# Two of six blocks by way of DRAM in all groups but the last, the written order up to there, and a last period in an order of its own

## The chip, the cores and the metric

The kernel runs on one core of a Trainium2 chip. The core has a matrix engine (TensorE, PE), a vector engine (VectorE, DVE), a scalar engine (ScalarE, ACT), GpSimd (POOL) and SyncE (SP), which issues nearly all DMAs here. The metric is the device time of one execution in microseconds; lower is better.

## The reference

```python
# attention: B, H, S, D = 4, 8, 768, 64; proj is 64 x 6
q_bucket = sum over 6 bits of (q @ proj > 0) * 2**bit      # k_bucket likewise
scores = q @ k.T / sqrt(D), -1e9 where q_bucket != k_bucket
attn = exp(scores - rowmax);  attn /= attn.sum(-1) + 1e-9
out = attn @ v
# mixture of experts: x = out as 3072 tokens x 512, E = 8, F = 1024
expert = argmax(x @ w_gate);  gate = softmax(x @ w_gate)[expert]
y[token] = gate * (maximum(x @ w1[expert], 0) @ w2[expert])
```

All arithmetic is in float32. A product of two float32 operands runs on the matrix engine in two passes, so a program instruction shows as two records; products of split operands (a high part xh and a rest xl, likewise whi and wlo) run in one.

## The kernel before

**Groups and blocks.** The 32 heads form 16 pairs, each pair two groups: group k = 0 to 31 has 384 queries (three parts jj of 128) of both heads hh of a pair, that is 6 blocks x = 2·jj + hh of 128 queries by 768 keys. A block passes through: S, its scores (PE, L237 and L238); X, the row maximum with the scores copied out (DVE, L248, L249); E, the exponential (ACT, L253); its transpose, keys on the partitions, into a tile `pt`; and the product with V. The transpose has two ways. T is six PE transposes (L277, halves a and b), each half copied from PSUM by K (ACT, L281). Blocks 2 and 3 (`AWAY`) of the groups in `MOVED` take the other: X writes them permuted into `pd`, O writes `pd` to DRAM (`moved`, eight DMAs for both blocks, L263), B reads it back as `pq` (L266), and U transposes it in squares on DVE into `pt` (L269). The part jj = 1 is just the blocks 2 and 3.

**Products with V.** A0, A1 and A2 are the products of a group's three parts, each 12 instructions (24 records, L294), all into one PSUM tile `o`; each part has its own tile pt0, pt1, pt2, of which pt0 has two buffers. Then follow EV (copy of `o`), SU and RC (sums), OT (transposes back, L320) and OM (L331). After the last group of a batch of eight, LG to SC route the batch's tokens: logits, argmax, slots, and a scatter of the token rows by POOL into `xs` in DRAM, grouped by expert.

**The order.** `ORDER` is a list of names with lags: period t emits each name for group t minus its lag, so that each engine's instructions stand in that order. A period emits the products of group t-1 (A0, A2, A1), the transposes of group t, and the scores of group t+1; N0 to N5 mark the six places 6t+n of a period, at which `marker` may add work. The list serves groups 2 to 27 (`START`, `END` = 28; `MOVED` = 2 to 27). Groups 0 and 1 and groups 28 to 31 are written step by step: step i handles block i mod 6 of group i div 6, `steps_of` emitting scores ahead and `PIECES` = {1: "1", 3: "2", 5: "0"} the products of the group before, one part at a time. The last group has code of its own, with the routing of the last two groups and the first products of the expert layer among it.

**Beside it.** For each pair LQ and LV load q, k and v (`qk`, `vt`), Q and K_ split them on POOL, and CP, CT, CR and CW form hash codes (PE, L155; DVE, L160) and copy their rows into q and k by DMA (L188). `prefill` clears an expert's rows of `xs` by one DMA of 910 KB from `zrow` (L122); `FILL` = 3, 5, 7, 9, 11, 23, 35, 47 are its places. At place 166 (`PICK`) the expert that comes first is chosen on DVE. At place 174 `weights_early` closes the pools of the early tiles and opens `wpa` (first expert's weights, whi and wlo) and `xep` (its first rows `xre`, its later rows `xrl`); then come its W1 in four loads of 512 KB (`wraw`), a cast on DVE (L758) and a subtraction on POOL (L761) for each, and four turns of `xre` (DVE, L722). SP issues a load when its `wraw` buffer (two of them) is free again.

**Expert layer.** After the last group, L792 forms the first expert's products: the part of `xre` (y = 0), then that of `xrl` (y = 1), which is loaded late. The other experts follow, double-buffered.

Of the kernel before, what the change touches and what calls it, by code (L numbers as in the profile page):

```python
# [18 lines left out]
P = 128  # L19
# [45 lines left out]
def lsh_attention_moe_kernel(ctx, tc, qkd, q2d, k2d, v, pjbd, wg, w1, w2, ident_in, tri_in, cols_in, eoff_in, ids_in, out):  # L65
# [28 lines left out]
    early, first, psa, in_order = ExitStack(), ExitStack(), ExitStack(), ExitStack()  # L94
    rawp = early.enter_context(tc.tile_pool(name="rawp", bufs=4, side="right"))
    pdp = early.enter_context(tc.tile_pool(name="pdp", bufs=2, side="right"))
    start = ExitStack()
    raw0 = start.enter_context(tc.tile_pool(name="raw0", bufs=2, side="right"))
    wpa = []
# [180 lines left out]
    def half_copy(t, pt, c):  # L280
        A.copy(out=pt[:, 3 * c:3 * c + 3], in_=t[:, 0:384].rearrange("p (c q) -> p c q", c=3))  # L281
# [55 lines left out]
    def route(b, g):  # L337
# [14 lines left out]
        def logits_out():  # L352
            (V.tensor_copy if (b, g) == (B - 1, 0) else A.copy)(out=lsb, in_=cell["lps"][:, 0:384])
# [73 lines left out]
    def last_route(sums, o):  # L427
# [7 lines left out]
        ohbs = gp.tile([P, 3, E], BF16, name="ohb")  # L435

        def chain(jj, pools):
# [104 lines left out]
    MOVED = range(2, 2 * NPR - 4)  # L542
# [8 lines left out]
    h0, h1 = ([raw0.tile([P, S], F32, name=n) for n in ("qr", "kr")] for hh in range(2))  # L551
# [23 lines left out]
    START, END = 2, 2 * NPR - 4  # L575

    def probs_t(pr, g, jj):
        if (pr, g, jj) not in pts:
            pts[(pr, g, jj)] = ptp.tile([P, 2, NB, P], F32, name=f"pt{jj}", bufs=PTBUFS[jj])
        return pts[(pr, g, jj)]  # L580
# [6 lines left out]
    def for_block(name, k, x, half):  # L587
# [5 lines left out]
        elif name == "X":  # L593
            soft[i] = fold(soft[i], x in AWAY and START <= k <= END, moves)
# [26 lines left out]
    def for_group(name, k):  # L621
        pr, g = divmod(k, 2)
        routed = pr % NPAIR == NPAIR - 1
        if name[0] == "A":
            if ("o", k) not in state:
                state["o", k] = ps_o.tile([P, 512], F32, name="o")
            av(pr, g, int(name[1]), state["o", k])
        elif name == "EV":
            av_evac(pr, g, state.pop(("o", k)), A.copy)
# [13 lines left out]
    PTBUFS = (2, 1, 1)  # L643
# [3 lines left out]
    def emit(name, k):  # L647
# [3 lines left out]
        if name[0] in "SXEOBUTK" and name[1:2].isdigit():  # L651
# [54 lines left out]
    def first_x(pool):  # L706

        n, n0 = SQS[0], E0 // SQ
        xr = [pool.tile([P, n0, RSEG], F32, name="xre"), pool.tile([P, n - n0, RSEG], F32, name="xrl")]
        xh = [pool.tile([P, NDC, x.shape[1] * SQ], F32R, name=f"xh{y}") for y, x in enumerate(xr)]  # L710
        xl = [pool.tile([P, NDC, x.shape[1] * SQ], F32R, name=f"xl{y}") for y, x in enumerate(xr)]
        xt = [pool.tile([P, E0], F32, name=f"xt{y}") for y in range(2)]

        def load(y):
            rows = rows_of_x(0, (0, E0)[y], (E0, SQS[0] * SQ)[y])
            for g in range(NG):
                SY.dma_start(out=xr[y][g * SQ:g * SQ + SQ], in_=rows[g])

        def early(c):

            if c < NDC:
                V.transpose(out=xt[c % 2].rearrange("p (i t) -> p i t", t=SQ), in_=xr[0][:, :, c * SQ:c * SQ + SQ])  # L722
            if c:
                A.copy(out=xh[0][:, c - 1], in_=xt[(c - 1) % 2])
# [601 lines left out]
```

## Time and profile before

| | us |
|---|---|
| three executions | 717.16, 719.38, 722.79 |
| median | 719.38 |
| profiled execution, its own time | 727.14 |
| its span on the core | 724.9 |
| mean granted PE clock of that span | 0.995 |

The profiled execution is 7.8 us above the median; 2.2 us of its own time lie outside the span. Times below are counted from the start of the span. Attention runs to 433.49, the last product with V; the rest is the expert layer.

### The profile page before, as it was taken

The numbers are of one execution on the slowest core, as the hardware profiler recorded it, in microseconds if no ns is written. First come the engines' busy times: TensorE is split into PE (matmuls) and PEld (weight loads), VectorE is DVE, ScalarE is ACT, GpSimd is POOL, SyncE is SP. The second block draws the span as 40 slices with busy tenths as digits, with TensorE's granted clock in tenths as the row PEclk, the third lists the DMA queues.
The fourth block names the chain that finished last, engine by engine and source line by source line (L and its number), as shares of the span: only waits on it lengthen the run. The fifth ranks groups of instructions, "written<-read, shape, count | busy, mean of one in ns | idle before, by whom it ended". The sixth has DMA issues, their size and how long they took to land.

```text
span 724.9 us, 16296 instructions
## 1 busy us (share of the span) xinstructions
PE 698.5 (96%) x5895; PEld 630.1 (87%) x5895; DVE 488.2 (67%) x1160; ACT 436.8 (60%) x935; POOL 384.4 (53%) x366
## 2 busy tenths in 40 slices
PE   6989989999999999999999989999999999999996
PEld 3878888888888888988878869999999999989894
DVE  6668777887878978788855656655565656564641
ACT  6877868678787778787778743433343435343440
POOL 2869437458744695476751612047383746537171
PEclk9999999999999999999999999999999999999999
DMA  8378758676766677667724306575646565757421
GB/s 280 91 226 248 221 143 262 207 208 200 223 193 180 186 242 209 172 179 214 212 70 123 118 16 162 158 182 152 175 155 172 153 174 156 202 138 212 146 77 41
DMA packets 88138, 124.58 MB, mean 172 GB/s; under 512 B 11078, under 2 KB 59750, under 8 KB 88048
## 3 DMA queue, kind: packets, MB, share of 16 engines
q1 hardware_dynamic: 83056, 110.76, 53.8%
q0 software_dynamic: 4992, 12.69, 5.0%
q8 instruction: 48, 0.79, 0.5%
q14 instruction: 42, 0.34, 0.2%
HBM read 80.61 MB, written 40.81 MB: 168 GB/s over the span
## 4 chain that ended last, share of the span: by engine, by line
PE 47%; issue 22%; POOL 13%; DMA 9%; DVE 4%; SPq 3%; ACT 1%; POOLq 0%; another core or an unknown queue 0%; DVEq 0%; ACTq 0%
PE o L294 15%; POOL y L1102 11%; PE t L277 10%; PE s L237 9%; PE s L238 8%; DMA pq<-moved 3%; DMA y<-yo,tags 2%; SPq L188 2%; POOL yo L1100 1%; PE t L155 1%; PE misc L320 1%; DMA qk<-qkd 1%; DVE pt L269 1%; DMA xr<-xs 1%; DVE p L248 1%
## 5 line engine op out<-in xcount | busy, mean ns | idle before, releaser
L281 ACT COPY pt<-t 128x384 f32<-128x384 f32 x280 | 122.8, 480 | 76.8 <-PE t L277 74.6
L248 DVE TENSOR_SCALAR_CACHE_REDUCE p<-s 128x768 f32<-128x768 f32 x138 | 131.3, 951 | 31.5 <-PE s L238 26.7
L237 PE MATMUL s<-k,q 128*128 128x512 f32 (+1 forms) x384 | 147.8, 385 | 1.7 <-DVE p L248 1.3
L294 PEld LDWEIGHTS o<-pt,vt 128*64 128x64 f32 x2304 | 125.1, 137 | 14.3 <-issue 11.5
L294 PE MATMUL o<-pt,vt 128*64 128x128 f32 x2304 | 136.0, 274 | 1.0 <-DVE pt L269 0.8
L253 ACT ACTIVATE p<-p,m 128x768 f32<-128x768 f32 x138 | 128.4, 937 | 3.2 <-DVE m L249 2.7
L238 PE MATMUL s<-k,q 76*128 76x512 f32 (+1 forms) x384 | 123.5, 343 | 2.2 <-DMA k<-cr 1.6
L277 PE MATMUL t<-ident,p 128*128 128x128 f32 x828 | 119.7, 274 | 2.4 <-ACT pt L281 1.6
L1102 POOL DMA_INDIRECT y<-yo,tags x89 | 102.9, 1156 | 25.2 <-issue 23.0
L277 PEld LDWEIGHTS t<-ident,p 128*128 128x128 f32 x828 | 94.6, 140 | 7.4 <-ACT pt L281 3.8
L237 PEld LDWEIGHTS s<-k,q 128*128 128x128 f32 x384 | 73.2, 191 | 25.4 <-issue 9.3
L1060 ACT ACTIVATE hh<-hps 128x352 fp32r<-128x352 f32 (+3 forms) x56 | 28.0, 500 | 105.6 <-PE hps L1074 87.4
L761 DVE TENSOR_TENSOR wlo<-wraw,whi 128x1024 fp32r<-128x1024 f32 x60 | 72.9, 1216 | 19.4 <-ACT whi L756 17.1
L238 PEld LDWEIGHTS s<-k,q 76*128 76x128 f32 x384 | 73.7, 192 | 11.8 <-DMA k<-cr 1.9
L1093 PE MATMUL hps<-hh,whi 128*128 128x448 f32 (+10 forms) x224 | 77.1, 344 | 1.5 <-ACT whi L756 1.2
L1093 PE MATMUL hps<-hh,wlo 128*128 128x436 f32 (+6 forms) x224 | 77.0, 344 | 1.4 <-issue 0.7
L1093 PE MATMUL hps<-hl,whi 128*128 128x436 f32 (+6 forms) x224 | 77.0, 344 | 0.2
L173 POOL CAST q<-qk 64x768 fp32r<-64x768 f32 x30 | 24.7, 823 | 95.9 <-DMA qk<-qkd 66.0
L1074 PE MATMUL hps<-xh,whi 128*128 128x352 f32 (+3 forms) x224 | 75.0, 335 | 0.0
L1074 PE MATMUL hps<-xh,wlo 128*128 128x428 f32 (+6 forms) x224 | 74.8, 334 | 0.0
L1074 PE MATMUL hps<-xl,whi 128*128 128x428 f32 (+6 forms) x224 | 74.8, 334 | 0.0
L1100 POOL TENSOR_TENSOR yo<-yt,tags 128x512 f32<-128x512 f32 (+3 forms) x25 | 23.4, 960 | 94.8 <-DVE yt L1095 94.7
(227 smaller groups left out, 1243.5 us busy)
## 6 DMA issues: line engine op xcount, KB each, us to landing
wraw<-w SPq DMA_DIRECT2D x64, 512.0 KB
moved<-pd SPq DMA_DIRECT2D x208, 96.0 KB
pq<-moved SPq DMA_DIRECT2D x52, 384.0 KB
qk<-qkd SPq DMA_DIRECT2D x30, 384.0 KB
xs<-zrow SPq DMA_DIRECT2D x8, 910.0 KB
vt<-v SPq DMA_DIRECT2D x16, 384.0 KB
xr<-xs SPq DMA_DIRECT2D x12, 178.8 KB
xr<-xs SPq DMA_DIRECT2D x8, 227.5 KB
```

What stands on the lines that cost most here:

```text
L237: PE.matmul(out=s[:, c0:c1], lhsT=q1[:, qs], rhs=k1[:, c0:c1], start=True, stop=False)
L238: PE.matmul(out=s[:, c0:c1], lhsT=q2[0:KM, qs], rhs=k2[0:KM, c0:c1], start=False, stop=True)
L248: V.tensor_scalar(out=to, in0=of, scalar1=-0.5 * BIG, scalar2=-BIG, op0=ALU.max, op1=ALU.max, accum_out=m[:, 0:1])
L253: A.activation(p, p, AF.Exp, bias=m[:, 1:2], scale=0.125, accum_out=sums[:, idx:idx + 1])
L277: PE.transpose(out=t[:, i * P:i * P + P], in_=p[:, kc * P:kc * P + P], identity=ident)
L281: A.copy(out=pt[:, 3 * c:3 * c + 3], in_=t[:, 0:384].rearrange("p (c q) -> p c q", c=3))
L294: PE.matmul(out=o[hh * D:hh * D + D, jj * P:jj * P + P], lhsT=vt[:, kc, hh * D:hh * D + D], rhs=pt[:, hh, kc], start=kc == 0, stop=kc == N ...
L761: loeng.tensor_tensor(out=lo[:, i:i + step], in0=cell["t"], in1=bf(hi[:, i:i + step]), op=ALU.subtract)
L1074: PE.matmul(out=hps[:, 0:w], lhsT=wt[:, c, fs], rhs=xt[:, c, 0:w], start=n == 0, stop=n == 3 * NDC - 1)
L1093: PE.matmul(out=yps[:, 0:w], lhsT=wt[:, f, ds], rhs=ht[:, 0:w], start=n == 0, stop=n == 3 * NFC - 1)
L1100: G.tensor_tensor(out=yo[:, 0:i1 - i0], in0=yt[:, i0:i1], in1=tags[:, i0:i1, 1:2].broadcast_to([P, i1 - i0, SEG]), op=ALU.mult)
L1102: rows_apart("out", G.indirect_dma_start(out=out_seg, out_offset=bass.IndirectOffsetOnAxis(ap=tags[:, i, 0:1].bitcast(I32), axis=0), in_=y ...
```

## The change

- `END` and `MOVED` reach to 31: groups 2 to 30 take the moved blocks, and the list runs to period 30. The step code for groups 28 to 31 is gone. The last period is a list of its own, `LAST`, which names each step with its group, the products of the last group (Z), the early logits (L), the last routing (C) and the first products of the expert layer (P). In group 31 blocks 2 and 3 are written to `pd` but transposed on PE.
- The tiles pt1 and pt2 become one, `pt` True, 256 queries wide with one buffer. In all groups but the last, A2 issues 12 products of 256 columns for both parts, and A1 nothing. In the step code of the first groups `PIECES` is {1: "20"}: all products of a group stand in step 1.
- `wpa` is open from the start; its tile `wlo` holds the raw first heads meanwhile. The first expert's rows, their turns and splits use the attention's own tiles (`xr`, `qk`, `cr`); `xrl` has a pool opened after attention. Its loads and splits have places of their own in `EXTRA`.
- LQ of the third pair's heads moves from steps 8 and 10 to step 1; `FILL` is 2, 3, 4, 5, 23, 35, 47, 53; `PICK` is 158.
- In the last period seven copies are on DVE (J) in place of ACT (K), EV of group 30 is on DVE, and the last routing's `s` tile is shared by two chains.

```diff
+LAST = """
+T4b:30 RC:29 U2:30 N0 T5a:30 X4:31 J4b:30 K4a:30 N1 T5b:30 J5a:30 J5b:30 X5:31 OT:29 T1a:31 A0:30 T1b:31 U3:30 OM:29 T0b:31 K1a:31 A2:30 J1b:31 N2 J0b:31 L0 E4:31 EV:30 T2a:31 T2b:31 J2b:31 L1 E5:31 T3a:31 LG:30 K2a:31 SU:30 L2 K3a:31 Z0 LS:30 T3b:31 RC:30 K3b:31 GH:30 T4a:31 C0 T4b:31 LW:30 K4b:31 TP:30 Z1 K4a:31 OH:30 OT:30 RX:30 T5a:31 C0 T5b:31 OM:30 C1 K5b:31 C0 RK:30 J5a:31 C0 Z2 RP:30 C2 C1 C2 P1 RR:30 N3 C0 P10 C1 C2 C1 C0 C1 C0 C2 SC:30 C2 P2 C1 C0 C0 C1 C2 C1 C0 C2 P10 C0 C2 C2 C1 C2 C2 P77 P19 P3 C1 C1
+"""
...
-    def av(pr, g, jj, o):
+    def av(pr, g, jj, o, n=1):
         vt = operands[pr][1]
-        pt = probs_t(pr, g, jj)
+        pt = probs_t(pr, g, jj) if n == 1 else pts[(pr, g, True)]
         for kc in range(NB):
             for hh in range(2):
-                PE.matmul(out=o[hh * D:hh * D + D, jj * P:jj * P + P], lhsT=vt[:, kc, hh * D:hh * D + D], rhs=pt[:, hh, kc],
+                PE.matmul(out=o[hh * D:hh * D + D, jj * P:jj * P + n * P], lhsT=vt[:, kc, hh * D:hh * D + D], rhs=pt[:, hh, kc],
                           start=kc == 0, stop=kc == NB - 1)
...
-    MOVED = range(2, 2 * NPR - 4)
+    MOVED = range(2, 2 * NPR - 1)
...
-    START, END = 2, 2 * NPR - 4
+    START, END = 2, 2 * NPR - 1
...
-    PTBUFS = (2, 1, 1)
+    PTBUFS = (2, 1)
...
-    FILL = (3, 5, 7, 9, 11, 23, 35, 47)
...
+    FILL = (2, 3, 4, 5, 23, 35, 47, 53)
...
+    PICK = 6 * (2 * NPR - NPAIR - 2) + 2
+    EXTRA = [(PICK, lambda: picks[0]()), (PICK + 1, lambda: picks[1]())]
+    EXTRA += [(172, first_weights)]
+    EXTRA += [(i, partial(load_first, x)) for x, i in enumerate((174, 176, 179, 182))]
+    EXTRA += [(i, partial(split_first, x)) for x, i in enumerate((178, 181, 184, 186))]
+    EXTRA += [(i, partial(at_first, x)) for x, i in enumerate((175, 176, 178, 180, 182, 184))]
...
-    PIECES = {1: "1", 3: "2", 5: "0"}
-    PREPARE = {2: (2, "Q0 Q1"), 3: (2, "CP CT K_0"), 5: (2, "CR K_1"), 6: (2, "CW0"), 7: (2, "CW1"), 8: (4, "LQ0"), 10: (4, "LQ1"),
-               168: (30, "Q0"), 169: (30, "CP CT Q1"), 170: (30, "K_0"), 171: (30, "CR CW0 K_1"), 172: (30, "CW1"), 174: (30, "LV")}
+    PIECES = {1: "20"}
+    PREPARE = {1: (4, "LQ0 LQ1"), 2: (2, "Q0 Q1"), 3: (2, "CP CT K_0"), 5: (2, "CR K_1"), 6: (2, "CW0"), 7: (2, "CW1")}
...
-    for t in range(-4, END + 3):
+    for t in range(-4, END):
...
+    for w in LAST.split():
+        if ":" in w:
+            name, k = w.split(":")
+            emit(name, int(k))
         else:
-            some_products(n)
+            last_piece(w)
```

Four places show how instructions move. A row is a line, an operation, its output and inputs, the input's size and, where it repeats, how often.

First steps, SP's queue, before:

```order
L815 DMA qr<-q2d 128x384
L122 DMA xs<-zrow 112x8x260 x2
L147 DMA vt<-v 128x768
L188 DMA q_296<-cr 12x384
L188 DMA k_298<-cr 12x384
```

and, eight rows on, before:

```order
L188 DMA k_302<-cr 12x384
L142 DMA qk<-qkd 128x768
L122 DMA xs<-zrow 112x8x260
L142 DMA qk<-qkd 128x768
L122 DMA xs<-zrow 112x8x260
L263 DMA moved_61<-pd 32x4x192 x4
```

and now:

```order
L841 DMA wlo<-q2d 128x384
L143 DMA qk<-qkd 128x768 x2
L123 DMA xs<-zrow 112x8x260 x4
L148 DMA vt<-v 128x768
L189 DMA q_298<-cr 12x384
L189 DMA k_300<-cr 12x384
```

The two loads of `qk` for the third pair stood behind three fills and eight code rows, and now stand ahead of all of them.

Period 28 on PE, from the transposes on (t are transposes, s scores, o products with V), before:

```order
L277 MATMUL t<-ident,p 128x128 x12
L320 MATMUL misc<-ident,ot 128x128 x3
L277 MATMUL t<-ident,p 128x128 x12
L294 MATMUL o<-pt_5733,vt 64x128 x12
L277 MATMUL t<-ident,pd 128x128 x6
L237 MATMUL s<-k_5263,q_5261 128x512
L238 MATMUL s<-k_5264,q_5262 128x512
L237 MATMUL s<-k_5263,q_5261 128x256
L238 MATMUL s<-k_5264,q_5262 128x256
L277 MATMUL t<-ident,pd 128x128 x6
L294 MATMUL o<-pt_5710,vt 64x128 x12
```

and now, the products of group 27 with what follows them:

```order
L295 MATMUL o<-pt_5179,vt 64x128 x12
L295 MATMUL o<-pt_5368,vt 64x256 x12
L238 MATMUL s<-k_4935,q_4933 128x512
L239 MATMUL s<-k_4936,q_4934 128x512
L238 MATMUL s<-k_4935,q_4933 128x256
L239 MATMUL s<-k_4936,q_4934 128x256
L278 MATMUL t<-ident,p 128x128 x3
```

The products of a group stand together, 12 of 128 columns and 12 of 256, in place of three parts among the next group's transposes, and no block of `pd` is transposed.

The last period on PE, its first part, before:

```order
L277 MATMUL t<-ident,p 128x128 x6
L294 MATMUL o<-pt_6183,vt 64x128 x12
L294 MATMUL o<-pt_6250,vt 64x128 x12
L237 MATMUL s<-k_5673,q_5671 128x512
L238 MATMUL s<-k_5674,q_5672 128x512
L237 MATMUL s<-k_5673,q_5671 128x256
L238 MATMUL s<-k_5674,q_5672 128x256
```

and now:

```order
L278 MATMUL t<-ident,p 128x128 x12
L321 MATMUL misc<-ident,ot 128x128 x3
L278 MATMUL t<-ident,p 128x128 x3
L295 MATMUL o<-pt_5710,vt 64x128 x12
L278 MATMUL t<-ident,p 128x128 x6
L295 MATMUL o<-pt_5884,vt 64x256 x12
L527 MATMUL misc<-ot,wg_sb 32x384 x3
L278 MATMUL t<-ident,pd 128x128 x6
```

Transposes of groups 30 and 31 now stand in a row with no scores between them, except for the products of group 30.

Period 29 on DVE (`cr<-xr` is a turn of the first expert's rows), now:

```order
L735 STREAM_TRANSPOSE cr<-xr 128x288
L249 TENSOR_SCALAR p,m<-s 128x768
L250 TENSOR_SCALAR m<-m 128x1
L332 TENSOR_TENSOR xr<-misc,inv 128x3x128
L270 STREAM_TRANSPOSE pt_5541<-pq 128x6x128
L249 TENSOR_SCALAR pd,m<-s 128x6x4x32
L250 TENSOR_SCALAR m<-m 128x1
L783 CAST whi<-wraw 128x1024
```

and the first expert's turn and cast in step code, before:

```order
L722 STREAM_TRANSPOSE xt_5912<-xre 128x288
L248 TENSOR_SCALAR p,m<-s 128x768
L249 TENSOR_SCALAR m<-m 128x1
L758 CAST whi<-wraw 128x1024
L248 TENSOR_SCALAR p,m<-s 128x768
```

The turns and casts now stand among the squares of the moved blocks in DVE's queue.

## Rows read from the trace of the kernel before

**Rows 1.** The page: engines by busy time, and the chain of waits by engine.

```profile
PE 698.5 (96%) x5895; PEld 630.1 (87%) x5895; DVE 488.2 (67%) x1160; ACT 436.8 (60%) x935; POOL 384.4 (53%) x366
...
PE 47%; issue 22%; POOL 13%; DMA 9%; DVE 4%; SPq 3%; ACT 1%; POOLq 0%; another core or an unknown queue 0%; DVEq 0%; ACTq 0%
```

**Rows 2.** Busy time by stretch (its bounds and length, then busy time and count of each engine, granted clock, share of the DMA engines, GB/s): from the products of group 1 to those of group 26; on to the last product with V; on to the first expert's second part; the rest.

```profile
49.97:363.71 313.74, 309.60 (x3283) 273.06 (x3282) 250.59 (x671) 246.80 (x577) 197.21 (x182) 1.00 0.71 204
363.71:433.49 69.78, 67.13 (x720) 56.49 (x716) 42.40 (x134) 49.34 (x119) 22.51 (x21) 1.00 0.26 78
433.49:448.98 15.49, 13.94 (x112) 13.56 (x110) 10.35 (x59) 3.85 (x13) 5.19 (x7) 1.00 0.45 150
448.98:724.90 275.92, 266.50 (x1513) 257.35 (x1511) 152.36 (x215) 101.33 (x152) 132.52 (x131) 0.99 0.54 154
```

**Rows 3.** The same view of one period of the list, and of one period of the step code.

```profile
200.54:212.81 12.27, 12.27 (x133) 10.81 (x132) 9.70 (x25) 10.20 (x25) 4.39 (x5) 1.00 0.70 212
387.26:400.76 13.50, 13.50 (x136) 11.93 (x135) 8.78 (x25) 11.40 (x28) 3.21 (x3) 1.00 0.59 165
```

**Rows 4.** Timeline of PE in that period of the list (start, duration, instruction): the products of a group, scores, one block's transposes, code products.

```profile
200.54 4.15 PE L294 MATMUL o<-pt,vt 128*64 128x128 f32 x72
204.62 0.50 PE L237 MATMUL s<-k,q 128*128 128x512 f32 x1
...
205.44 0.49 PE L277 MATMUL t<-ident,p 128*128 128x128 f32 x3
...
206.47 0.82 PE L277 MATMUL t<-ident,p 128*128 128x128 f32 x6
207.04 0.48 PE L237 MATMUL s<-k,q 128*128 128x512 f32 x1
...
212.02 0.85 PE L155 MATMUL t<-qk,pj 128*32 128x384 f32 x8
```

**Rows 5.** Timeline of PE where the step code takes over (in brackets the idle time before an instruction, and what ended it).

```profile
370.43 0.93 PE L277 MATMUL t<-ident,p 128*128 128x128 f32 x6 [0.30 <-ACT pt L281]
...
373.53 0.43 PE L294 MATMUL o<-pt,vt 128*64 128x128 f32 x2
374.81 1.52 PE L294 MATMUL o<-pt,vt 128*64 128x128 f32 x22 [0.85 <-DVE pt L269]
```

**Rows 6.** Timeline of PE in the last group and just behind its last product with V.

```profile
425.18 0.85 PE L349 MATMUL t<-ot,wg_sb 128*32 128x384 f32 x8
425.97 0.55 PE L277 MATMUL t<-ident,p 128*128 128x128 f32 x3
...
432.03 1.53 PE L294 MATMUL o<-pt,vt 128*64 128x128 f32 x24
...
435.57 0.41 PE L457 MATMUL t<-wg_sb,ot 128*128 128x32 f32 x2 [1.55 <-DVE ot L451]
```

**Rows 7.** One line's instructions each: the turns of the first expert's rows and the casts of its W1 on DVE, the subtractions on POOL (count, then shortest, median and longest in ns, then first and last start in us).

```profile
L722 DVE STREAM_TRANSPOSE xt<-xre x4: 468/468/473, 394.2 to 404.9; 128x288 f32<-128x288 f32 x4
...
L758 DVE CAST whi<-wraw x4: 682/684/892, 395.6 to 407.7; 128x1024 fp32r<-128x1024 f32 x4
...
L761 POOL TENSOR_TENSOR wlo<-wraw,whi x4: 2392/2409/2416, 396.5 to 408.7; 128x1024 fp32r<-128x1024 f32 x4
```

**Rows 8.** Timeline of PE at the third pair's code products.

```profile
39.86 0.83 PE L155 MATMUL t<-qk,pj 128*32 128x384 f32 x2
42.79 0.85 PE L155 MATMUL t<-qk,pj 128*32 128x384 f32 x6 [2.10 <-DMA qk<-qkd]
```

**Rows 9.** SP's queue ahead of them: the third pair's two loads.

```profile
33.62 0.52 SPq L142 DMA_DIRECT2D qk<-qkd  x1
...
34.66 0.55 SPq L142 DMA_DIRECT2D qk<-qkd  x1
```

**Rows 10.** ACT's busy time in the stretch before them (bounds, length, busy time, count, clock, DMA share, GB/s).

```profile
24.00:38.20 14.20, 12.27 (x30) 1.00 0.50 147
```

**Rows 11.** Instructions by line, out and in, count, then total busy us and mean ns, then idle time before them: the products with V, the code products (four of which lie side by side in the array), the weight loads of the products with V, the copies of transposes on ACT.

```profile
L294 PE MATMUL o<-pt,vt 128*64 128x128 f32 x2304 | 136.0, 274 | 1.0 <-DVE pt L269 0.8 <-issue 0.2
...
L155 PE MATMUL t<-qk,pj 128*32 128x384 f32 x112 | 12.8, 498 | 2.1 <-DMA qk<-qkd 2.1
...
L294 PEld LDWEIGHTS o<-pt,vt 128*64 128x64 f32 x2304 | 125.1, 137 | 14.3 <-issue 11.5 <-DVE pt L269 1.1 <-DVE mark L683 0.2
...
L281 ACT COPY pt<-t 128x384 f32<-128x384 f32 x280 | 122.8, 480 | 76.8 <-PE t L277 74.6 <-issue 1.1 <-PE s L238 1.0
```

**Rows 12.** SP's queue: the eight writes of the moved blocks behind the fill at 85.84, and the same in the period of rows 4, with the reads back there; four loads of expert weights.

```profile
89.74 9.05 SPq L263 DMA_DIRECT2D moved<-pd  x8
...
205.51 4.07 SPq L263 DMA_DIRECT2D moved<-pd  x8
...
210.25 2.01 SPq L266 DMA_DIRECT2D pq<-moved  x2
...
398.96 12.53 SPq L752 DMA_DIRECT2D wraw<-w  x4
```

**Rows 13.** What ended the idle time of DVE just before its turns of moved blocks, L269 (us in all, times).

```profile
  PE o L294: 13.4, 18
...
  DMA pq<-moved: 1.9, 2
```

**Rows 14.** Timeline of DVE: the first turns of the later rows.

```profile
447.64 0.57 DVE L702 STREAM_TRANSPOSE xt<-xrl 128x160 f32<-128x160 f32 x2 [1.22 <-DMA xrl<-xs]
```

More of the change, by code (lines that the diff above doesn't have):

```diff
@@ L92, in lsh_attention_moe_kernel @@
     wst = ctx.enter_context(tc.tile_pool(name="wst", bufs=2))
[L94 to L99, printed above, removed]
+    first, psa, in_order = ExitStack(), ExitStack(), ExitStack()
+    wpa = ctx.enter_context(tc.tile_pool(name="wpa", bufs=1, side="right", reuse_waits="tile"))
+    rawp = first.enter_context(tc.tile_pool(name="rawp", bufs=4, side="right"))
+    pdp = att.enter_context(tc.tile_pool(name="pdp", bufs=2, side="right"))
     opp = att.enter_context(tc.tile_pool(name="opp", bufs=4))
@@ L626, in for_group @@
                 state["o", k] = ps_o.tile([P, 512], F32, name="o")
[L627 removed]
+            jj = int(name[1])
+            if jj == 2 and ("A1", k) not in done:
+                done.add(("A1", k))
+                av(pr, g, 1, state["o", k], 2)
+            else:
+                av(pr, g, jj, state["o", k])
         elif name == "EV":
[L629 removed]
+            av_evac(pr, g, state.pop(("o", k)), A.copy if k < END - 1 else V.tensor_copy)
         elif name == "SU":
@@ L704, in square, with first_x, load @@
         return lambda: low.tensor_tensor(out=xl[:, c], in0=xt, in1=bf(xh[:, c]), op=ALU.subtract)
[L706 to L715, printed above, removed]
+    def first_x():
+        xre = xrp.tile([P, 3, NG, RSEG], F32, name="xr").rearrange("p j g w -> p (j g) w")[:, 0:E0 // SQ]
+        halves = [rawp.tile([P, S], F32, name="qk")[:, 0:2 * E0].bitcast(F32R).rearrange("p (c t) -> p c t", c=2) for _ in range(4)]
+        xh, xl = ([halves[2 * y + c // 2][:, c % 2] for c in range(NDC)] for y in range(2))
+        xt = [bf(codep.tile([P, 384], F32R, name="cr"))[:, 0:E0] for _ in range(2)]
+        def load():
+            rows = rows_of_x(0, 0, E0)
@@ L723, in early, with rest_of_x @@
             if c:
-                A.copy(out=xh[0][:, c - 1], in_=xt[(c - 1) % 2])
-                G.tensor_tensor(out=xl[0][:, c - 1], in0=xt[(c - 1) % 2], in1=bf(xh[0][:, c - 1]), op=ALU.subtract)
-        load(0)
-        return xr, xh, xl, xt, load, early
+                A.copy(out=xh[c - 1], in_=xt[(c - 1) % 2])
+                G.tensor_tensor(out=xl[c - 1], in0=xt[(c - 1) % 2], in1=bf(xh[c - 1]), op=ALU.subtract)
+        x_parts.append((xh, xl))
+        return load, turn
+    def rest_of_x(pool):
+        n = SQS[0] - E0 // SQ
+        xr = pool.tile([P, n, RSEG], F32, name="xrl")
+        xh, xl = (pool.tile([P, NDC, n * SQ], F32R, name=x) for x in ("xh1", "xl1"))
+        xt = [pool.tile([P, n * SQ], F32, name=f"xt{y}") for y in range(2)]
+        rows = rows_of_x(0, E0, SQS[0] * SQ)
+        for g in range(NG):
+            SY.dma_start(out=xr[g * SQ:g * SQ + SQ], in_=rows[g])
+        x_parts.append([[t[:, c] for c in range(NDC)] for t in (xh, xl)])
+        return xr, xh, xl, xt
@@ L1162, in lsh_attention_moe_kernel @@
         sort_experts()
-        x_first[0][4](1)
+        rest = rest_of_x(first.enter_context(tc.tile_pool(name="xep", bufs=1, side="right", reuse_waits="tile")))
         load_weights(1)
```

203 lines of the change are left out of this document (77 added, 126 removed).

## The prediction

> **What bounds the kernel.** I read the page first: PE is busy for 698.5 of 724.9 us, and no other engine for more than 67% [rows 1]. The chain of waits gives PE 47% and issue 22%, the latter mostly PE's own sequence too. So an edit pays only by taking work off PE or by closing one of its few gaps. Where these lie the stretches show [rows 2]: the 25 periods from group 1 to group 26 leave PE idle for 4.1 of 313.7 us, the four groups behind them for 2.7 of 69.8, the expert layer for 9.4 of 275.9. Most of what the change can win is therefore PE work, with the caution that records which wait for an operand inside a run also count as busy.
>
> Then I compared one period of the list with one of the step code [rows 3]. PE is full in both, but the list needs 12.27 us, of which 0.79 are the code products that only every other period has (212.02 to its end at 212.81 [rows 3, 4]), so 11.48 without them; the step code needs 13.50. There ACT is busy for 11.40 in place of 10.20, since it copies six transposed blocks and not four. The timeline of the list's period prices the pieces on PE [rows 4]: products of a group 4.08 (200.54 to 204.62), scores of a block 0.82 (204.62 to 205.44), transposes of a block 0.57 when nothing holds them (206.47 to 207.04).
>
> **The change, part by part.** Everything is summed against the profiled execution's own 727.14 us, of which 2.2 lie outside the span; it stands 7.8 above the median of the three, and I carry the difference over to the median.
>
> *The last four groups: -9.4.* Before, products of group 26 to last product: 363.71 to 433.49, 69.78 us. After, periods 28 to 30 are of the list and without code products (pair 15's stand ahead of group 26's products in both versions): 3 x 11.49 = 34.5. Then the products of group 29, 4.1, and the last period, counted from the order: two blocks of scores 1.64, 45 transposes at 0.095 4.3, the products of group 30 4.1 and of group 31 4.4 (three parts at 1.46, as in 432.03 to 433.49 [rows 2, 6]), logits 0.8 (425.18 to 425.97 [rows 6]), and some 2.2 for the small products, transposes back and routing beside them. That is 17.4, and the floor is 56.0. Of the 13.8 us below today's time, 6 x 0.57 = 3.4 are the transposes of six blocks, 2.7 idle time (some at the takeover, where a product waits 0.85 for a turned block that DVE reaches late [rows 5]), and the remaining 7.7 is stretching: transposes that wait for PSUM tiles which ACT empties, and products in three separate parts.
>
> To the floor I add waits. DVE is busy for 9.70 of the period with code products [rows 3], whose own share on DVE the last periods lack. Period 29 adds three turns at 0.47 and a cast at 0.68, together 2.1, which makes at most 11.8; period 30 adds a turn and three casts at 0.68 to 0.89, some 2.7, which makes at most 12.4 [rows 7], against PE's 11.49. DVE thus becomes as long as PE in two periods. I take +2.3 for the three, between nothing (the queues let work slide from one period to the next) and 6 (they repeat the step code's 13.50). In the last period the transposes of groups 30 and 31 stand close together, almost without scores between them; the copy of three takes 0.48 [rows 11] for 0.29 of PE, but seven of the fifteen copies move to DVE. I take +2.1, between nothing and 5. So 60.4, hence -9.4, with ends at -13.8 and -3.
>
> *First steps: -2.0.* The third pair's code products stop for 2.10 us on the load of q and k; from 39.86 to 42.79, two records of the pair that should take 0.2 (0.79/8 each) cost 2.93 [rows 8]. Its two loads are issued at 33.62 and 34.66, behind code rows and fills [rows 9]. Now they stand ahead of the fills and get several us more. The 2.6 us of gap go, unless a fill delays the second pair's code rows instead: four fills now stand ahead of these, two before. Further, putting all products into step 1 leaves steps 2 to 6 with 0.82 + 0.57 = 1.39 of PE against an exponential and two copies of 0.48 on ACT [rows 11], which was busy for 12.27 of 14.20 before [rows 10]. This gives up to 1 us back, half of what ACT had free there. I take -2.0, between -2.6 and +1.
>
> *Merged products: -0.9.* Twelve instructions of 256 columns replace 24 of 128 in 31 groups. A part of 24 records takes 1.46 alone and 1.36 within a run (4.08/3): 57 ns a record. Code products of 384 columns, four side by side, take 0.79/8 = 99 ns each [rows 4, 11]; 128 columns, two side by side as here, would take 66 by that. So no time is lost between records that merging could save, and I take 0.03 us a group, of at most the 0.10 between 1.46 and 1.36 (3.1 in all). The last of the two moved squares, a turn of 0.97, must now be there 1.36 us into the run; U3 mostly waits for the products before to free the tile, not for its rows [rows 13], so it costs nothing there. If that cover is gone, a period loses up to 0.97. The K copies of blocks 4 and 5 now also wait for the merged tile, which comes free at the end of a run as pt1 did: nothing.
>
> A rule of the Trainium skill speaks otherwise: "TensorE: Matmul & The Clock Gate", Part 3 on packing, "What overlaps and what doesn't", says that weight loads overlap running products only where the row group differs. By it each dropped weight load would free PE for its own time. The row has 57 ns from record to record of products that show 274 ns each, with loads of 137 ns beside them [rows 4, 11], so that the loads do overlap here; the sum by it is the third rival.
>
> *Choice of the expert in period 26, fill in period 8: +1.0.* The choice's small DVE instructions leave the takeover, where PE waited 0.85 for DVE [rows 5], for a full period of the list: +0.7, most of that gap again, between 0 and 1.5. The fills move to early steps but for the one at 53, in a period of the list, +0.3, between 0 and 2.5.
>
> *Behind the last product: 0.* Before, PE waits 1.55 for the routing [rows 6], and the later rows' first turn comes at 447.64, as soon as their load has landed [rows 14], 1.3 us before the products need them (448.98 [rows 2]). This chain stays, its pieces reordered: 0, between -1.5 and +1.5. The expert layer itself: 0.
>
> Sum: -9.4 - 2.0 - 0.9 + 1.0 = **-11.3**; 727.1 becomes 715.8, and the median 719.4 becomes **708**.
>
> **The rivals.**
>
> *1. ACT and DVE hold the end.* If the last period waits for its copies twice as long as I take (17.4 + 4.2 = 21.6) and periods 28 to 30 run at DVE's 12.4 plus its waits for scores, 13, then 3 x 13 + 4.1 + 21.6 = 64.7, a gain of 5.1; the start then gives only 0.6, as ACT holds it too. For it: DVE's 12.4 for 11.49, and PE's wait for a copy at the takeover [rows 5]. Against it: PE is wholly busy in the list's periods although ACT has 10.20 and DVE 9.70 of 12.27 [rows 3]. In sum -5.1 - 0.6 - 0.9 + 1.0 = -5.6: **714**.
>
> *2. The other side: one SP queue.* In periods 29 and 30 four loads of 512 KB, four rows loads and waits for the splits on POOL (2.4 us each [rows 7]) stand between the writes and reads of the moved blocks in SP's queue. Before, these loads had SP nearly to themselves, and SP still spent 12.53 on four of them [rows 12]. A load that waits for its buffer holds the read `pq` behind it; U then comes late, and behind U, in order on DVE, the maxima and so PE's scores. Precedent: behind a fill the eight writes took 9.05 in place of 4.07 [rows 12]. The slack: in the period of rows 4 the reads are issued from 210.25 to 212.26, and the products that need them begin a period of 11.5 after 212.81; with 1.36 for the first part, less 0.97 for the turn and some 2.4 for the transfer, 10 us are left [rows 3, 4, 12]. From there on each further microsecond counts in full. That speaks against it: the 5.0 of a fill still fit. It ends slower than before once the three periods lose more than 13.6 us (69.8 + 1.9 of the other terms - 58.1, floor and last period's waits), 4.5 each. Priced at 20, a 5.0 for each of the four loads on top of the slack, the stretch takes 78.1, which is +8.3; less 1.9, +6.4: **726**. "DMA: Bandwidth & Descriptors" of the Trainium skill, "Issuing engines are not separate DMA queues", has all issuers share 16 engines; here their share in the list's periods is 0.70 [rows 3], so there is room for the loads as such.
>
> *3. Weight loads cost PE time.* 24 records of loads fewer, at 54 ns each (125.1/2304 [rows 11]), in 31 groups would be 40 us: **668**. Against it stands the spacing of 57 ns.
>
> **How the numbers follow.** About 1% (7 us) is what a measurement of this kernel can tell from no change. Forecast 0.64 (701 to 712.5), first rival 0.21 (711 to 718), second 0.12 (720 to 735), third 0.03. The range 701 to 717 leaves out the second and third and the tails. Faster by over 1% (below 712.2): 0.62 + 0.05 + 0.03 = 0.70; within 1%: 0.02 + 0.16 + 0.04 = 0.22; slower by over 1% (above 726.6): 0.08.
>
> **What would show it.** Right: products of groups 26 to 29 at 11.5 to 12.3 us apart; last product 60 to 61 us after group 26's start; no PE gap at the third pair's code products; a group's products (48 records) in 4.0 to 4.1. Rival 1: PE gaps in the last periods ended by ACT `pt` or DVE. Rival 2: DVE idle before its squares until `pq`, and PE until DVE, in periods 29 and 30. Wrong altogether: a lower granted clock, or a merged run well under 3.9 us.

## The result, and the profile after

The changed kernel takes 726.95 us (median of six runs, 724.80 to 729.42) against 719.84 for the kernel before, a ratio of 1.0085 with a 95% interval from 1.0056 to 1.0115: slower by some 0.9%, where 708 was forecast and 701 to 717 was the range. Its profiled execution took 727.62 us, a span of 725.7 at a mean granted clock of 0.977, the one before 727.14, 724.9 and 0.995. In all six runs the mean granted clock lies between 0.977 and 0.982.

The stretches of the kernel after, which answer to [rows 2] (bounds, length, busy time and count by engine, granted clock, share of the DMA engines, GB/s):

```profile
47.28:359.05 311.77, 308.64 (x2682) 249.03 (x2681) 252.00 (x678) 246.67 (x577) 187.98 (x173) 1.00 0.71 209
359.05:426.17 67.12, 62.88 (x561) 49.95 (x557) 47.17 (x127) 41.82 (x100) 26.63 (x24) 0.95 0.53 154
426.17:443.14 16.97, 14.15 (x112) 13.67 (x111) 10.71 (x69) 4.15 (x14) 6.26 (x8) 1.00 0.37 126
443.14:484.52 41.38, 41.36 (x192) 40.03 (x193) 20.16 (x31) 12.95 (x21) 0.40 (x2) 0.71 0.51 129
484.52:725.70 241.18, 233.87 (x1321) 227.02 (x1319) 133.55 (x185) 88.58 (x132) 135.62 (x129) 1.00 0.54 155
```

The last of [rows 2], divided in the same way: from the later part of the first expert to the first products of the second, and on.

```profile
448.98:479.14 30.16, 30.13 (x193) 28.87 (x192) 19.15 (x30) 12.62 (x20) 0.40 (x2) 1.00 0.72 171
479.14:724.90 245.76, 236.37 (x1321) 228.48 (x1319) 133.21 (x185) 88.71 (x132) 132.12 (x129) 0.99 0.52 152
```

| stretch | before | after | difference | predicted |
|---|---|---|---|---|
| start to products of group 1 | 49.97 | 47.28 | -2.7 | -2.0 |
| to products of group 26 | 313.74 | 311.77 | -2.0 | +0.1 |
| to the last product with V | 69.78 | 67.12 | -2.7 | -9.4 |
| to the first expert's later part | 15.49 | 16.97 | +1.5 | 0 |
| to the second expert | 30.16 | 41.38 | +11.2 | 0 |
| to the end | 245.76 | 241.18 | -4.6 | 0 |

Attention ends 7.3 us earlier, and the first expert gives back 12.7. I do not put the last row down to the change: it compares one execution each, and in that of before PE stood still near 640 and 672, late in the expert layer, while the same code takes 238.92 in an experiment below. This is also why the profiled executions are level while the medians differ by 7.1.

Timeline of PE after (in brackets idle time, and what ended it), at its three stops, that is, where it stands still (the second is a pair):

```profile
380.85 0.49 PE L278 MATMUL t<-ident,p 128*128 128x128 f32 x3
383.93 0.50 PE L238 MATMUL s<-k,q 128*128 128x512 f32 x1 [2.60 <-DVE p L249]
...
384.84 5.80 PE L295 MATMUL o<-pt,vt 128*64 128x128 f32 x48
...
404.01 0.51 PE L238 MATMUL s<-k,q 128*128 128x512 f32 x1 [0.67 <-DVE pd L249]
...
406.05 2.39 PE L278 MATMUL t<-ident,p 128*128 128x128 f32 x9 [0.73 <-ACT pt L282]
...
440.02 0.29 PE L818 MATMUL t<-qk,wlo 128*128 128x288 f32 x1
443.14 0.34 PE L818 MATMUL s<-xh,whi 128*128 128x160 f32 x1 [2.82 <-ACT xh L716]
```

The granted clock around the first and behind the third (columns bounds, length, PE busy, clock, DMA share, GB/s):

```profile
382.00:384.00 2.00, 0.07 (x1) 1.00 1.06 382
384.00:386.00 2.00, 2.00 (x22) 0.92 0.87 221
386.00:388.00 2.00, 2.00 (x18) 0.50 0.93 360
...
440.00:443.10 3.10, 0.32 (x3) 1.00 0.57 143
443.10:446.10 3.00, 2.94 (x14) 0.60 0.96 249
446.10:466.10 20.00, 20.00 (x91) 0.50 0.47 133
466.10:470.10 4.00, 4.00 (x18) 0.81 0.00 0
```

After each stop the granted clock falls from 1.00 to 0.50 (0.54 from 406 to 408 behind the pair), from 2.4 to 1.2 GHz, although PE is then busy; the products of group 28 take 5.80 instead of 4.12 in group 29, and the first expert's later part runs at half speed for more than 20 us.

What PE waited for is on DVE and SP. DVE's first turn of the expert's rows, period 29, and SP's queue beside it:

```profile
382.54 0.48 DVE L735 STREAM_TRANSPOSE cr<-xr 128x288 f32<-128x288 f32 x1 [3.42 <-DMA xr<-xs]
```
```profile
375.65 0.36 SPq L777 DMA_DIRECT2D wraw<-w  x1
376.35 1.94 SPq L729 DMA_DIRECT2D xr<-xs  x4
378.38 1.90 SPq L264 DMA_DIRECT2D moved<-pd  x4
380.48 0.36 SPq L777 DMA_DIRECT2D wraw<-w  x1
381.06 3.17 SPq L264 DMA_DIRECT2D moved<-pd  x4
...
438.58 1.98 SPq L751 DMA_DIRECT2D xrl<-xs  x4
```

The rows were issued at 376.35, and DVE, which works in order, stood for 3.42 us until they were there, with the maxima behind it. The later rows (`xrl`), which follow the last scatter of tokens, were issued at 438.58, 12.4 us after the last product; before it was 10.4 (443.86 and 433.49). PE's early part ends 14.1 us after the last product (at 440.32, 2.82 ahead of 443.14) in place of 15.4 (448.91), mainly since the wait of 1.55 of [rows 6] is gone. Before, the first later operand was cast some 0.9 us ahead of the product that reads it, and now 2.4 us after the early part's end:

```profile
448.02 0.56 ACT L703 CAST xh<-xt 128x160 fp32r<-128x160 f32 x2 [7.01 <-DVE xt L702]
448.91 0.23 PE L792 MATMUL s<-xh,whi 128*128 128x160 f32 x1
```
```profile
442.76 0.55 ACT L716 CAST xh<-xt 128x160 fp32r<-128x160 f32 x2 [10.71 <-DVE xt L715]
```

So PE ran out of work.

### The profile page after: what moved, and what is told of

It reads as the page before. It is cut to its first block, busy times and chain, and to the rows that moved or that the text cites. A ratio compares the mean times of both kernels' runs of the same rounds, so it can differ in the third digit from the quotient of the medians.

```text
span 725.7 us, 14799 instructions
## 1 busy us (share of the span) xinstructions
PE 702.5 (97%) x5115; PEld 609.0 (84%) x5115; DVE 495.9 (68%) x1171; ACT 429.5 (59%) x918; POOL 389.1 (54%) x367
## 4 chain that ended last, share of the span: by engine, by line
PE 43%; issue 23%; POOL 14%; DMA 9%; DVE 4%; SPq 4%; ACT 2%; POOLq 0%; another core or an unknown queue 0%; DVEq 0%; ACTq 0%
PE o L295 14%; POOL y L1083 11%; PE t L278 10%; PE s L238 8%; PE s L239 7%; DMA y<-yo,tags 2%; DMA pq<-moved 2%; SPq L189 2%; POOL yo L1081 2%; DMA moved<-pd 2%; DMA xr<-xs 2%; PE misc L321 1%; PE t L156 1%; DVE p L249 1%; SPq L264 1%
## 5 line engine op out<-in xcount | busy, mean ns | idle before, releaser
L282 ACT COPY pt<-t 128x384 f32<-128x384 f32 x261 | 115.0, 480 | 77.5 <-PE t L278 71.7
L249 DVE TENSOR_SCALAR_CACHE_REDUCE p<-s 128x768 f32<-128x768 f32 x132 | 125.5, 951 | 18.0 <-PE s L239 15.1
L295 PE MATMUL o<-pt,vt 128*64 128x128 f32 (+1 forms) x1560 | 135.2, 328 | 0.1
L295 PEld LDWEIGHTS o<-pt,vt 128*64 128x64 f32 x1560 | 96.6, 138 | 35.7 <-issue 10.1
L254 ACT ACTIVATE p<-p,m 128x768 f32<-128x768 f32 x132 | 122.5, 935 | 3.4 <-DVE m L250 3.3
L1083 POOL DMA_INDIRECT y<-yo,tags x89 | 104.9, 1178 | 25.2 <-issue 22.9
L278 PE MATMUL t<-ident,p 128*128 128x128 f32 x792 | 116.2, 276 | 2.0 <-ACT pt L282 1.9
L278 PEld LDWEIGHTS t<-ident,p 128*128 128x128 f32 x792 | 92.0, 142 | 6.0 <-ACT pt L282 4.2
```

What stands on the lines that cost most here:

```text
L249: V.tensor_scalar(out=to, in0=of, scalar1=-0.5 * BIG, scalar2=-BIG, op0=ALU.max, op1=ALU.max, accum_out=m[:, 0:1])
L254: A.activation(p, p, AF.Exp, bias=m[:, 1:2], scale=0.125, accum_out=sums[:, idx:idx + 1])
L278: PE.transpose(out=t[:, i * P:i * P + P], in_=p[:, kc * P:kc * P + P], identity=ident)
L295: PE.matmul(out=o[hh * D:hh * D + D, jj * P:jj * P + n * P], lhsT=vt[:, kc, hh * D:hh * D + D], rhs=pt[:, hh, kc], start=kc == 0, stop=kc ...
L1083: rows_apart("out", G.indirect_dma_start(out=out_seg, out_offset=bass.IndirectOffsetOnAxis(ap=tags[:, i, 0:1].bitcast(I32), axis=0), in_=y ...
```

## The experiments

Each comparison is with the kernel before on the same chip in the same set of runs. The sets stand on different chips or at different times (medians of before 721.66, 714.89 and 721.98), so kernels of different sets are compared by their stretches.

**First set: PE's stops and the clock.** Theory A: the stops and the clock behind them cost the time. Theory B: it is the loads beside the later part, and DVE's or SP's excess of work in the last periods.

The gap filled:

```diff
+    FILLERS = 40
...
                 hs = first_h
+                for _ in range(FILLERS):
+                    PE.matmul(out=first_h[0][:, E0:SQS[0] * SQ], lhsT=w1_first[0][0][:, 0, 0:P], rhs=x_parts[0][0][0][:, 0:SQS[0] * SQ - E0], start=True, stop=True)
                 for f, done in first_products(1):
```

> The changed kernel with 40 products of 160 columns put on PE between the first expert's early part and its later part; they read operands that are there, write columns that the later part overwrites, and change no result. Theory A (PE's 2.8 us without work at 440.2 is what halves the granted clock behind it): the later part starts as late as now, at about 443, but runs at 2.4 GHz, 11.1 us in place of 20.7, and the products behind it 19.0 in place of 20.7; the time falls by about 11, to 716. Theory B (the later part is slow for another reason, as the loads beside it): no change, 727.

Measured: 715.53 us, 0.9926 of before (0.9892 to 0.9960). Timeline of PE, and the stretches behind it:

```profile
440.19 4.59 PE L1170 MATMUL s<-qk,whi 128*128 128x160 f32 x40
444.62 0.28 PE L819 MATMUL s<-xh,whi 128*128 128x160 f32 x1
```
```profile
444.62:474.30 29.68, 29.68 (x195) 28.78 (x194) 18.22 (x27) 11.97 (x19) 0.40 (x2) 1.00 0.69 166
```

Counted from the last product with V, the later part now begins 1.4 us later than in the changed kernel (18.4 and 17.0), so the filling products lengthen the wait, and the time still falls by 11: the stretch of 41.38 takes 29.68 at a clock of 1.00 with its loads unchanged. In all seven runs the mean granted clock is 0.994 to 0.997. The clock explains the 11; theory B falls for this part.

The turns one place later:

```diff
-    EXTRA += [(i, partial(at_first, x)) for x, i in enumerate((175, 176, 178, 180, 182, 184))]
+    EXTRA += [(i, partial(at_first, x)) for x, i in enumerate((175, 178, 180, 182, 184, 185))]
```

> The changed kernel with the four turns of the first expert's rows one place later each (places 178, 180, 182, 184 and 185 in place of 176, 178, 180, 182 and 184), their load left where it is. Theory A (DVE, which works in order, waits 3.4 us for these rows and holds the maxima behind it, PE stops for 2.6 us and its clock falls): the stop at 381 goes, with 2.6 us and some 1.7 of clock; about 723. Theory B (DVE's excess work or the queue of SP sets these periods; the wait only moves on to the next turn of a moved block): no change, 727.

Measured: 725.24 us, 1.0044 (1.0027 to 1.0062): 3.0 less than the changed kernel by the two ratios, and 1.7 by the stretch from group 26 to the last product (65.4 in place of 67.1), where A expected 4. The stop of 2.60 is gone, and the products of group 28 come 11.47 us after those of group 27 in place of 14.35. But two stops follow in the next period, and the clock behind them is 0.50 for some 6 us:

```profile
387.20 0.51 PE L238 MATMUL s<-k,q 128*128 128x512 f32 x1 [0.82 <-DVE pd L249]
389.44 0.50 PE L238 MATMUL s<-k,q 128*128 128x512 f32 x1 [0.93 <-DVE pd L249]
```

The wait was partly moved on, as B had it.

Both edits together:

> The changed kernel with both edits, the 40 products in the gap and the turns one place later. Theory A: the two gains add up, about 15; 712, faster than the kernel before by 1%. Theory B: 727. If the rows come a little earlier to the end of attention, the filler may be a little short or long (1 us).

Measured: 713.86 us, 0.9891 (0.9872 to 0.9909); in the third set, as a control, 715.81, 0.9921 (0.9885 to 0.9956). It is faster than the kernel before, by 0.8 to 1.1%, and so than the changed one. What still holds DVE in period 29 is a write of a moved block, whose `pd` the next maximum wants:

```profile
385.19 0.96 DVE L249 TENSOR_SCALAR_CACHE_REDUCE pd<-s 128x768 f32<-128x768 f32 x1 [3.10 <-DMA moved<-pd]
```

The converse, a gap in the kernel before:

```diff
                 for wt, xt in ((wh, xh), (wh, xl), (wl, xh)):
-
+                    if y == 0 and f > 1 and xt is xl:
+                        n += 1
+                        continue
                     w = c1 if n else c2
```

> The kernel before with the products of the rest xl left out in the early part of the first expert for six of its eight column blocks (24 products of 288 columns, 3.2 us of PE; the output lacks these terms). PE then ends the early part some 3 us before the later rows are there. Theory A: PE stands still for about 3 us, the clock halves behind that, and although 3.2 us of work are gone the time rises by about 11, to 731. Theory B (a stop of this length does not change the clock): no change, 720.

Measured: 731.07 us, 1.0135 (1.0110 to 1.0160). With 3.2 us of work taken away, the kernel is slower by 9.4, and the mean granted clock is 0.977 to 0.981 in all four runs. PE's stop, and the stretches behind it:

```profile
444.34 0.34 PE L794 MATMUL s<-xh,whi 128*128 128x160 f32 x1 [2.89 <-ACT xh L703]
```
```profile
444.34:485.75 41.41, 41.39 (x192) 40.02 (x193) 20.16 (x31) 12.98 (x21) 0.40 (x2) 0.71 0.53 131
485.75:724.67 238.92, 233.32 (x1321) 226.94 (x1319) 133.54 (x185) 88.52 (x132) 134.72 (x129) 0.99 0.54 156
```

The same stretch takes 41.41 here as in the changed kernel, without any of the change. By both kernels, a stop of PE of 2.8 to 2.9 us at this place costs 11 us beyond itself.

**Second set: the terms of the sum, on the kernel with both edits.** Before: 714.89. The rows and the first two loads of weights issued earlier:

```diff
-    EXTRA += [(i, partial(load_first, x)) for x, i in enumerate((174, 176, 179, 182))]
-    EXTRA += [(i, partial(at_first, x)) for x, i in enumerate((175, 178, 180, 182, 184, 185))]
+    EXTRA += [(i, partial(load_first, x)) for x, i in enumerate((172, 173, 179, 182))]
+    EXTRA += [(i, partial(at_first, x)) for x, i in enumerate((173, 178, 180, 182, 184, 185))]
```

> The kernel with both edits (filler, later turns), and the load of the first expert's rows at place 173 in place of 175 and the first two loads of its weights at 172 and 173 in place of 174 and 176, so that none of them stands ahead of the writes of the moved blocks of group 29 in SP's queue. With both edits DVE still waited 3.1 us at 382 until a write of `pd` had landed, and those eight writes were issued over 5.9 us behind the first expert's loads. Theory A (the queue of SP delays the writes, their buffer holds DVE): that wait goes, DVE catches up, and the time falls by 2 to 3, to 711. Theory B (DVE's excess work in these periods sets them, the wait is only its slack): no change, 714.

Measured: 714.54, 0.9985 (0.9957 to 1.0013), and the stretch from group 26 to the last product is 69.0 in place of 64.3. The wait for `pd` is gone, but the loads now stand ahead of the last pair's code rows, and PE waits for these:

```profile
378.87 0.47 PE L239 MATMUL s<-k,q 76*128 76x512 f32 x1 [2.88 <-DMA k<-cr]
381.93 0.77 PE L239 MATMUL s<-k,q 76*128 76x512 f32 x1 [1.46 <-DMA k<-cr]
```

The profiled execution, 716.46, is on the slow side of ten (709.95 to 717.35). Neither theory's number came: what the loads hold up in SP's queue was another of its members, and the place I chose for them was no better.

The parts apart again:

```diff
                 done.add(("A1", k))
-                av(pr, g, 1, state["o", k], 2)
+                av(pr, g, 1, state["o", k])
+                av(pr, g, 2, state["o", k])
```

> The kernel with both edits, with the parts 1 and 2 of a group's products as 12 products of 128 columns each again, side by side in one run, where the change has 12 of 256. By the prediction's term (little time is lost between records) the merge is worth 0.9, at most 3.1: 715, at most 717. By the rule that a weight load holds the products up unless the row group differs it would be worth 40: 754.

Measured: 713.25, 0.9980 (0.9952 to 1.0007), with its neighbours. A group's products take 4.08 us as 72 records and 4.05 as 48, the median of 25 groups each, counted to the start of the next record, so the merge gives 0.03 a group, 0.9 in all, too little for the comparison to show. No weight load's time was lost with the parts, in place of the 40 us that 754 stands for.

```profile
379.85 4.15 PE L295 MATMUL o<-pt,vt 128*64 128x128 f32 x72
```
```profile
396.74 4.12 PE L295 MATMUL o<-pt,vt 128*64 128x128 f32 x48
```

In this trace PE also stopped for 0.80, 0.73 and 1.25 us from 385 on, at half clock behind that, and the last stretch took 66.2; one trace cannot tell whether the parts are the reason.

The first steps' loads and fills as before:

```diff
-    FILL = (2, 3, 4, 5, 23, 35, 47, 53)
+    FILL = (3, 5, 7, 9, 11, 23, 35, 47)
...
-    PREPARE = {1: (4, "LQ0 LQ1"), 2: (2, "Q0 Q1"), ...
+    PREPARE = {2: (2, "Q0 Q1"), ..., 8: (4, "LQ0"), 10: (4, "LQ1")}
```

> The kernel with both edits, with the third pair's loads at steps 8 and 10 and the fills at 3, 5, 7, 9, 11, 23, 35 and 47 again. By the prediction's term the loads and fills of the first steps are worth 2.6 less what the one piece in step 1 costs, which stays: 716.5. A rival (the third pair's loads were only the last of several waits there): 714, no change.

Measured: 712.90, 0.9964 (0.9937 to 0.9991). As a whole it cannot be told from its neighbours; by the trace the products of group 1 start at 49.27, against 46.2 to 47.7 in the ten profiles of kernels with the change's first steps (46.73 with both edits). That is 2.5 for the loads and fills.

The casts on POOL:

```diff
-        w1_first.append(chunks(w1, first_expert, NDC, F, 0, hieng=V, loeng=G))
+        w1_first.append(chunks(w1, first_expert, NDC, F, 0, hieng=G, loeng=G))
```

> The kernel with both edits, with the four casts of the first expert's weights on POOL in place of DVE (2.9 us of DVE's time in periods 29 and 30, where it is busy for nearly all of 386 to 399). Theory B (DVE's excess sets these periods): about 2 less, 712. Theory A (the queue of SP and what DVE waits for): no change, 714, or a little more if POOL's splits come late and hold up the loads behind them.

Measured: 711.51, 0.9956 (0.9932 to 0.9980), the lowest of its set, though its interval overlaps its neighbours'. The last stretch takes 62.5 in place of 64.3, while DVE still waits 2.93 for `pd`. Where that code is unchanged, the stretch took 64.3, 64.2 and 63.7 in three traces, so the casts are worth 1.2 to 1.8 by one trace: B's excess of work is there, and the wait for the writes beside it.

**Third set: the loads apart.** Before: 721.98. On the kernel with both edits:

```diff
-    EXTRA += [(172, first_weights)]
-    EXTRA += [(i, partial(load_first, x)) for x, i in enumerate((174, 176, 179, 182))]
+    EXTRA += [(162, first_weights)]
+    EXTRA += [(i, partial(load_first, x)) for x, i in enumerate((164, 169, 179, 182))]
```

> The kernel with both edits (filler of 40, later turns), and the first two loads of the first expert's weights at places 164 and 169 in place of 174 and 176, so that they no longer meet its rows and the writes of the moved blocks; the rows stay at 175. With both edits the share of the DMA engines is over 1 from 380 to 384, the rows take 6 us to land, and DVE waits 3.1 us for the write of `pd`. Theory A (what SP has issued at once in period 29 fills the DMA engines, the writes land late and hold DVE): the wait falls to about 1 and the stretch from group 26 to the last product from 64.3 to about 62; the time falls by about 2 against the kernel with both edits. Theory B (DVE's excess): no change against it.

Measured: 712.69, 0.9885 (0.9813 to 0.9957), against 0.9921 for both edits alone; the intervals overlap. The last stretch takes 62.9 against 64.2 in the same set, and DVE's waits for the writes are

```profile
382.93 0.96 DVE L249 TENSOR_SCALAR_CACHE_REDUCE pd<-s 128x768 f32<-128x768 f32 x1 [1.53 <-DMA moved<-pd]
...
398.89 0.96 DVE L249 TENSOR_SCALAR_CACHE_REDUCE pd<-s 128x768 f32<-128x768 f32 x1 [2.16 <-DMA moved<-pd]
```

The first is half of 3.1, the second was 2.45 in the control. By this one trace the first two loads would be worth 0.9 to 1.4. It is not shown that they are part of the cause: with the loads at the same places in the next run, which has the casts on POOL as well, DVE's first wait is 2.57, and with them at the old places it is 2.65 in the run with the first steps undone.

> The same as the one before, with the casts of the first expert's weights on POOL and 27 filling products in place of 40. The 40 took 4.4 us, 1.4 longer than the later rows needed, so 13 fewer give 1.4 if the clock stays at 2.4 GHz; the casts gave 1.7 of the last stretch (64.3 to 62.5). With the loads apart: 4 to 5 under the kernel with both edits, and faster than the kernel before by more than 1%.

Measured: 713.87, 0.9892 (0.9857 to 0.9927), not better than the loads apart alone and 1.9 below both edits, where 4 to 5 were expected. The last stretch is the shortest of all, 61.3, and the later part starts 1.45 earlier, but it takes 11.85 in place of 10.88, its first products standing 0.2 to 0.3 us apart where a turned part begins, in place of 0.11; and this profiled execution lost some 7 us behind the first expert against the one before. One place is in a late expert, where PE waited for weights and the clock was 0.83 from 660 to 670:

```profile
661.59 0.49 PE L1075 MATMUL hps<-hh,whi 128*128 128x340 f32 x1 [1.88 <-ACT whi L782]
```

The control with both edits:

> The kernel with both edits again, for the comparison on this chip: 0.989 of the kernel before, as it had; or, as the chip of the second comparison has it (its neighbours stood at 0.996 to 0.998 there), 0.996.

The edit is that of the first set. Measured: 715.81, 0.9921 as above; it lies between the two expectations.

## Why the prediction was wrong

The direction was wrong, and the likeliest case did not come. The second rival's number, 726, came, but by luck: it put +8.3 on the last four groups, which measured -2.7, and nothing on the first expert, which gave back 12.7. Step by step:

- **Behind the last product, 0 ± 1.5: the step that failed.** It measured +12.7: 1.5 of waiting and 11.2 of clock. I had read that the later rows come 1.3 us before they are needed and PE's 1.55 us of waiting ahead of that, and did not put the two together: PE's early part ended at 448.91, less than 0.9 us after the first later operand was there. Now the early part ends 1.3 us sooner after the last product, and the path by way of routing, scatter and load takes 12.4 us in place of 10.4. The difference, less that margin, is the stop of 2.82. The term had the chain as unchanged and allowed 1.5 us either way, with no price for the clock behind a stop. The first and fourth experiments, one on each kernel, show that the clock behind it costs four times as much. "A lower granted clock" stood in the prediction only as a last remark, without a price, though the trace of the kernel before had an example at 672, in its expert layer.
- **The last four groups, -9.4: mis-sized.** It measured -2.7, so 6.7 are missing. Up to the products of group 29 (397.98) the stretch took 38.9 in place of 36.8 (34.5 + 2.3), and from there on 28.2 in place of 23.6 (4.1 + 17.4 + 2.1): the larger part, 4.6, is missing in the last period. The floor was about right where nothing waits: 11.44 for period 28. Periods 29 and 30 took 14.35 and 13.14, and that excess, 2.9 and 1.7, is the 2.60 us stop behind DVE's turn of rows that had not landed and the half clock on the products of group 28 (5.80 for 4.12). The prediction priced that turn at its own 0.47 and the wait for its rows at nothing. In the last period PE stops for 0.67 and 0.73 and the clock falls again, after DVE has waited for a write of a moved block:

```profile
402.99 0.96 DVE L249 TENSOR_SCALAR_CACHE_REDUCE pd<-s 128x768 f32<-128x768 f32 x1 [3.09 <-DMA moved<-pd]
```

With both edits the clock stays up there, but the last period from the products of group 29 on still takes 26.8, with a stop of 1.61 behind DVE's copies, and 25.2 at the least (casts on POOL); no experiment took this period apart. The first rival's excess of DVE is there, at 1.2 to 1.8 by one trace. The second rival's waits on what SP issues are there too; the experiments do not settle what they are worth.
- **Room for the loads: refuted.** I argued from a share of 0.70 that the DMA engines had room. Where the expert's loads meet the moved blocks the share is above 1 (1.06 from 382 to 384, in the rows of the clock above), and the first expert's rows took some 6 us to land.
- **First steps, -2.0: right,** 2.7 in the two traces, 2.5 by undoing; the code products run without a stop. In the other execution of the kernel before (the one with the gap) the products of group 1 start at 48.32, not 49.97, so the size is known to about 1.
- **Merged products, -0.9: right** to the digit, 0.03 a group, and the third rival is out.
- **Choice and fill, +1.0: too high or covered.** The periods of groups 1 to 26 fell by 2.0 against +0.1; between executions of one code this stretch varies by as much (310.95 and 313.74 for the kernel before), so it is not settled.
- **The base.** I carried the difference over from an execution 7.8 above the median. Its excess lies in the late experts (245.76 against 238.92), not in the part that changes, so the difference of two profiles and that of two medians need not agree: 0.5 and 7.1 here.

A gain is recovered with filler work and later turns: attention ends at 423.6 against 433.5, and the sum is 1.1% and 0.8% below the kernel before in two sets. In the set between them, the kernels with both edits and one more change are 0.2 to 0.4% below it, so the size is not settled. Of the forecast 9.4, 5.5 are then there (64.3), and 8.5 with casts on POOL and loads apart (61.3), by one trace each.

What no experiment settled is why the scatter's path lengthens by 2 us. The traces show where it begins. The first scatter, of group 30's rows, starts 1.1 us ahead of the last product's end in the kernel before (432.39 and 433.49) and 1.2 behind it now (427.40 and 426.17), each time 0.5 us after the start of the DVE instruction that writes the factors of these rows. In `LAST` that step, RR:30, stands behind the copy of the last product's result (the first C2), which waits for PE; before, it stood ahead of that copy:

```profile
431.88 0.23 DVE L413 RECIPROCAL xr<-mx 128x12 f32<-128x12 f32 x1
432.39 1.06 POOL L418 DMA_INDIRECT xs<-xr,slot  x1 [3.74 <-DVE lg L461]
435.22 0.29 DVE L451 COPY ot<-o 128x128 f32<-128x128 f32 x1 [1.93 <-remote]
```
```profile
426.21 0.29 DVE L457 COPY ot<-o 128x128 f32<-128x128 f32 x1 [0.54 <-PE o L295]
426.89 0.23 DVE L414 RECIPROCAL xr<-mx 128x12 f32<-128x12 f32 x1
427.40 1.06 POOL L419 DMA_INDIRECT xs<-xr,slot  x1 [2.98 <-DVE lg L467]
```

How much of the 2 us this order costs is not shown; DVE also waits there for 3.2 us while POOL scatters. Open too is how long the clock stays low after a stop: 3 to 7 us in attention and some 23 in the expert's later part.

## What to carry to other kernels

Where a change shortens the stretch ahead of a join, ask what PE has in hand until the other path arrives; where the two ends lie within 1 us, as here, the gain can become a stop. A stop of PE is to be priced with the clock behind it (here 11 us behind one of 2.8), and work without use can be cheaper than a stop. A load that is moved into a busy period needs its landing time from that period's DMA share, and its first reader should stand behind that in an in-order queue.

## What the runs showed of the hardware

- The granted clock halved after stops of PE of 2.60, 2.71, 2.77, 2.82, 2.88 and 2.89 us in these traces. Shorter ones went either way. After 0.67 and 0.73, or 0.82 and 0.93, 2 us apart, it halved; after 0.73 and 0.74 at the same distance, in the kernel with the gap filled, it stayed at 1.00, as it did after 0.85, 0.73 and 0.32 within 5 us with both edits. After single ones of 1.55 [rows 6] and 2.10 [rows 8] it stayed at 1.00; at the one of 1.88 in a late expert it halved.
- Behind the stop in front of the first expert's later part it stayed at 0.50 for some 23 us with PE busy all the time, in the changed kernel and in the one before with a gap alike (that stretch took 41.38 and 41.41, in place of 30.16 before and 29.68 with the stop filled), while after the stops in attention it was back within 3 to 7 us.
- Dropping 24 weight loads a group, which the trace shows at 54 ns each, gave PE 0.03 us: 72 records in 4.08 us, 48 in 4.05.
